# A fused adaLN attention block: engine order from a list scheduler, 4-head sets, exponentials in groups of three and two banks

## The chip, the cores and the metric

One core of a Trainium2 chip. The metric is device time in microseconds (us) of one execution; lower is better. The kernel before has a median of 1135.11 us over three runs (1132.73 to 1136.46). Engines: PE is TensorE (PEld its weight loads), ACT is ScalarE, DVE is VectorE, POOL is GpSimd, SP is SyncE, which here only issues transfers. Some words: PSUM is the memory that TensorE writes to, here in banks of 512 columns; an eviction copies a result out of it; the stationary is the operand that a weight load puts into the array, whose largest form in these profiles has 128 rows and 128 columns (`128*128`); a row or column group is, in these kernels, a strip of 32 of these; the granted clock is the share of full speed that the profile records for TensorE.

## The reference, cut to what matters

```python
# x: 1 x 2048 x 640, 32 heads of 20, gated MLP of 1536, all bfloat16
mod = silu(c) @ w_mod                       # six vectors: sa, ca, ga, sb, cb, gb
h = layernorm(x) * (1 + ca) + sa
q, k, v = split(h @ wqkv)                   # 32 heads x 20
o = softmax(q @ k.T / sqrt(20)) @ v         # 32 x 2048 x 2048 exponentials
x = x + ga * (o @ wo)
h = layernorm(x) * (1 + cb) + sb
x = x + gb * (((h @ w_gate) * (h @ w_up)) @ w_down)
```

The 134 million exponentials go through ScalarE: in the kernel before, one instruction of 128 x 1536 of them lasts 1.45 us alone and follows the last after 1.347 us back to back, and that sets the floor. The heads are small: 20 of the 128 rows of the TensorE array are enough for one head's scores.

## The kernel before

Heads are taken three at a time, in 11 sets. One step is one key tile of 128 for one set and 512 queries: three score matmuls side by side in row groups of the array, one exponential over three PSUM banks, three matmuls with the values (PV) side by side in column groups. The profile has 0.39 us for the three score matmuls together and 0.39 us for the three of PV (at 700.85 and 701.17 us). Each head's 20 rows are padded with zeros to 32, and the score matmul contracts all 32.

```python
SETS = [tuple(range(i, min(i + 3, H))) for i in range(0, H, 3)]
VW = 24                                     # one ones column, 20 values, padding
...
fn = lambda e, ...: e.matmul(
    ps_all[:, bs * 3 + i, :],
    KT_sb[32 * s:32 * s + 32, sg, kt * 128:(kt + 1) * 128],      # 32 rows x 128 columns
    QT_sb[32 * s:32 * s + 32, sg, cq * 512:(cq + 1) * 512],
    tile_position=(32 * s, 0))
...
fn = lambda e, ...: e.activation(Pbuf[:, sl, 0:nh * 512], ps_sflat[bs][:, 0:nh * 512],
                                 ACT.Exp, scale=SCALE)
```

All other matmuls (projections, and for the 512 queries before: out-projection and MLP) are put between the steps. In a step without any, a matmul of no use keeps TensorE occupied:

```python
xs.filler = lambda e: e.matmul(ps_all[:, BXW, :], KT_sb[0:32, 0, 0:128], QT_sb[0:32, 0, 0:512],
                               tile_position=(0, 0))
...
if used == 0:
    if self.filler is not None and step >= self.round_end_step + 2 and self.cur is None:
        self.pe.ins(lambda e, f=self.filler: f(e), waits=...)
```

The softmax here doesn't subtract the row's maximum and nothing guards it: scores larger than these inputs give would overflow.

## Time and profile before

| | us | how to read it |
|---|---|---|
| median of three runs | 1135.11 | |
| span of the profiled run | 1138.6 | first to last instruction |
| until the first exponential | 91.4 | head: load, modulation, layer norm, projections |
| exponentials | 969.5 | stream; 921 at the pace of ScalarE, 48.5 of stalls |
| after the last exponential | 77.7 | tail: the last queries' out-projection and MLP |

The lines that carry this are in the prediction. Two more will matter. The first is from the slices of the page of the kernel before: the TensorE clock that was granted, in tenths, in 40 slices of the span. The second is from its costliest groups: the score matmuls, with busy time, the mean of one in ns, and the idle time before them.

### The profile page before, as it was taken

How to read it: one execution, taken by the hardware profiler on the slowest of the kernel's cores; microseconds unless marked ns; L12 is line 12 of the kernel's file. 1: busy time of each engine (PE TensorE's matmuls, PEld its weight loads, DVE VectorE, ACT ScalarE, POOL GpSimd, SP SyncE). 2: the span in 40 equal slices, each digit the busy share in tenths (PEclk: the TensorE clock that was granted, in tenths of full speed). 3: DMA queues.
4: the chain of work that ended last, by engine and by line, in shares of the span. 5: the costliest groups of instructions: out<-in, count | busy, mean ns of one | idle time of the engine just before them, and what ended most of it. 6: DMA issues, size and time to landing. Idle time of an engine off the chain costs nothing.

```text
span 1138.6 us, 14720 instructions
## 1 busy us (share of the span) xinstructions
PE 952.1 (84%) x6035; PEld 293.7 (26%) x6095; DVE 390.4 (34%) x690; ACT 969.7 (85%) x752; POOL 37.8 (3%) x52
## 2 busy tenths in 40 slices
PE   1677898899998888888997898889987888889778
PEld 0331222222222222222322222223222222223434
DVE  2741322344323333332114333321123333322475
ACT  1559999999999899999999999999987999999200
POOL 7000000000000000000000000000000000000000
PEclk9788999999989889898989779999977899989889
DMA  8100001000022001100230011100400011100422
GB/s 295 57 1 1 1 1 30 1 1 1 1 75 53 1 12 45 37 13 6 68 78 1 1 30 41 35 1 18 133 1 1 12 36 35 24 6 20 126 64 64
DMA packets 80418, 40.59 MB, mean 36 GB/s; under 512 B 64544, under 2 KB 80032, under 8 KB 80352
## 3 DMA queue, kind: packets, MB, share of 16 engines
q1 hardware_dynamic: 77328, 32.29, 11.0%
q10 hardware_dynamic: 2624, 4.92, 1.2%
q0 software_dynamic: 400, 2.46, 0.6%
q8 instruction: 48, 0.79, 0.3%
q14 instruction: 18, 0.15, 0.0%
HBM read 37.03 MB, written 2.62 MB: 35 GB/s over the span
## 4 chain that ended last, share of the span: by engine, by line
PE 39%; ACT 29%; issue 16%; DVE 13%; POOL 2%; another core or an unknown queue 0%; ACTq 0%; POOLq 0%
ACT Pbuf L1146 26%; PE ps_all L1159 9%; PE ps_all L1130 9%; PE ps_all L724 7%; PE ps_all L959 3%; PE ps_all L1036 3%; PE ps_all L1073 3%; PE ps_all L1049 2%; PE ps_all L746 2%; DVE OT L1183 2%; DVE KT_sb L734 1%; DVE QT_sb L734 1%; ACT hT L620 1%; PE ps_all L852 1%; DVE xn L990 1%
## 5 line engine op out<-in xcount | busy, mean ns | idle before, releaser
L1146 ACT ACTIVATE Pbuf<-ps_all 128x1536 bf16<-128x1536 f32 (+1 forms) x704 | 928.9, 1526 | 40.6 <-PE ps_all L1130 39.4
L1130 PE MATMUL ps_all<-QT_sb,KT_sb 32*128 32x512 bf16 x2048 | 296.1, 412 | 73.1 <-ACT Pbuf L1146 49.5
L1159 PE MATMUL ps_all<-Pbuf,V_sb 128*24 128x512 bf16 x2048 | 294.1, 412 | 9.0 <-DVE OT L1183 8.8
L1130 PEld LDWEIGHTS ps_all<-QT_sb,KT_sb 32*128 32x128 bf16 x2048 | 68.9, 92 | 323.7 <-ACT Pbuf L1146 244.2
L1159 PEld LDWEIGHTS ps_all<-Pbuf,V_sb 128*24 128x24 bf16 x2048 | 67.2, 89 | 189.4 <-issue 169.0
L959 PE MATMUL ps_all<-wo_sb,Oc 128*128 128x320 bf16 x352 | 76.7, 344 | 13.9 <-DVE h2T L1005 11.7
L1036 PE MATMUL ps_all<-h2T,wgst 128*128 128x512 bf16 x216 | 71.9, 410 | 9.8 <-DVE hprod L1054 4.4
L1073 PE MATMUL ps_all<-wd_sb,hprod 128*128 128x320 bf16 x384 | 72.5, 313 | 6.2 <-DVE wd_sb L934 5.4
L1049 PE MATMUL ps_all<-h2T,wust 128*128 128x512 bf16 x228 | 71.8, 398 | 4.9 <-DVE gsb L1041 3.4
L1183 DVE STREAM_TRANSPOSE OT<-ps_all 96x512 f32<-96x512 f32 (+1 forms) x44 | 31.3, 711 | 118.3 <-PE ps_all L1159 118.3
L1041 DVE COPY gsb<-ps_all 128x512 f32<-128x512 f32 x48 | 32.9, 685 | 89.8 <-PE ps_all L1036 82.4
L1054 DVE TENSOR_TENSOR hprod<-ps_all,gsb 128x512 bf16<-128x512 f32 x48 | 32.8, 684 | 89.9 <-PE ps_all L1049 78.8
L968 DVE TENSOR_TENSOR xck<-ps_all,xck 128x320 bf16<-128x320 f32 x32 | 15.3, 486 | 121.5 <-PE ps_all L959 121.5
L746 PE MATMUL ps_all<-Wv,hT 128*128 128x384 bf16 x160 | 40.6, 394 | 12.9 <-ACT hT L620 12.9
L1083 DVE TENSOR_TENSOR xck<-ps_all,xck 128x320 bf16<-128x320 f32 x32 | 15.5, 484 | 98.5 <-PE ps_all L1073 98.5
L724 PE MATMUL ps_all<-hT,Wk 128*128 128x512 bf16 x147 | 43.5, 394 | 6.3 <-DVE KT_sb L734 2.9
L724 PE MATMUL ps_all<-hT,Wq 128*128 128x512 bf16 x149 | 42.8, 383 | 5.3 <-issue 1.0
L734 DVE CAST KT_sb<-ps_all 128x512 bf16<-128x512 f32 x32 | 22.1, 691 | 67.1 <-PE ps_all L724 67.1
L959 PEld LDWEIGHTS ps_all<-wo_sb,Oc 128*128 128x128 bf16 x352 | 29.2, 106 | 51.8 <-issue 22.7
L734 DVE CAST QT_sb<-ps_all 128x512 bf16<-128x512 f32 x32 | 22.1, 692 | 56.0 <-PE ps_all L724 53.9
L1073 PEld LDWEIGHTS ps_all<-wd_sb,hprod 128*128 128x128 bf16 x384 | 30.3, 99 | 38.4 <-issue 17.9
L934 DVE TENSOR_TENSOR wd_sb<-wd_sb,mods_b 128x640 bf16<-128x640 bf16 x48 | 39.0, 813 | 0.0
(68 smaller groups left out, 433.5 us busy)
## 6 DMA issues: line engine op xcount, KB each, us to landing
wd_sb<-in_B_w_down_dram SPq DMA_DIRECT2D x4, 1920.0 KB, 9.4
wgst<-in_B_w_gate_dram SPq DMA_DIRECT2D x48, 160.0 KB, 2.7
wust<-in_B_w_up_dram SPq DMA_DIRECT2D x48, 160.0 KB, 2.8
wmod_sb<-in_w_mod_dram ACTq DMA_DIRECT2D x4, 1200.0 KB, 13.9
x<-in_A_x_dram SPq DMA_DIRECT2D x4, 640.0 KB, 7.1
xck<-in_A_x_dram SPq DMA_DIRECT2D x4, 640.0 KB, 4.3
out_dram<-xck SPq DMA_DIRECT2D x16, 160.0 KB, 1.8
wraw<-in_A_wqkv_dram POOLq DMA_DIRECT2D x5, 480.0 KB, 5.9
```

The lines of the kernel that those rows point to most:

```text
L724: fn = lambda e, b, kt=kt: e.matmul(psbank(b), Wx[:, kt, sg, :], hT[:, tc, kt, :], start=(kt == 0), stop=(kt == KT - 1))
L734: eve = dve.ins(lambda e: e.tensor_copy(dst[:, sg, tc * 512:(tc + 1) * 512], psbank(b)), inc=c_ev, waits=w)
L746: fn = lambda e, b, kt=kt: e.matmul(psbank(b)[:, 0:ncol], hT[:, tc, kt, (t % 4) * 128:(t % 4 + 1) * 128], Wv[:, kt, cc * ncol:(cc + 1) * n ...
L934: ev_wdp_l[0] = dve.ins(lambda e: e.tensor_tensor(wd_sb[:, fc, :], wd_sb[:, fc, :], mods_b[:, 2, :], ALU.mult), inc=c_ev, waits=[ev_wdl])
L959: fn = lambda e, b, j=j, tl=tl, nch=nch: e.matmul(ps_all[:, b, 0:320], Ocq[:, j, tl * 128:(tl + 1) * 128], wo_sb[:, j, nch * 320:(nch + 1) ...
L1036: fn = lambda e, b, kt=kt, stg=stg: e.matmul(psbank(b), wgst[:, stg, kt, :], h2T[:, kt, :], start=(kt == 0), stop=(kt == KT - 1))
L1049: fn = lambda e, b, kt=kt, stg=stg: e.matmul(psbank(b), wust[:, stg, kt, :], h2T[:, kt, :], start=(kt == 0), stop=(kt == KT - 1))
L1073: fn = lambda e, b, fc=fc, tl=tl, nch=nch: e.matmul(ps_all[:, b, 0:320], hprod[:, fc, tl * 128:(tl + 1) * 128], wd_sb[:, fc, nch * 320:(nc ...
L1130: fn = lambda e, bs=bs, i=i, sg=sg, s=s, cq=cq, kt=kt: e.matmul(ps_all[:, bs * 3 + i, :], KT_sb[32 * s:32 * s + 32, sg, kt * 128:(kt + 1) ...
L1146: fn = lambda e, sl=sl, nh=nh, bs=bs: e.activation(Pbuf[:, sl, 0:nh * 512], ps_sflat[bs][:, 0:nh * 512], ACT.Exp, scale=SCALE)
L1159: fn = lambda e, i=i, h=h, sl=sl, kt=kt: e.matmul(ps_all[32 * i:32 * i + VW, BO, :], V_sb[:, kt, h * VW:(h + 1) * VW], Pbuf[:, sl, i * 512 ...
L1183: ev_t1 = dve.ins(lambda e, rows=rows: e.transpose(OT[0:rows, :], ps_all[0:rows, BO, :]), inc=c_at, waits=[ev_pv[g], st["onorm"]] + extra)
```

## The change

The intent: fewer and fuller instructions, and an order of every engine that is worked out at build time by a list scheduler which knows the engines' durations. Heads go in eight sets of four; score tiles flow in one queue into groups of three banks (A) and two banks (B) in turn; queries and keys are projected packed (five blocks of 128 rather than eight padded ones) and laid out by small transfers from SBUF to SBUF ("relays"); the out-projection contracts 5 blocks of 128 instead of 11 sets; the modulation is folded into evictions and weights; the head of the program does only what the first scores need. The scores contract 20 rows now, the values' stationary has 21 columns, and there is no filler. The core of the diff (2,680 lines, all else cut):

```diff
-    SETS = [tuple(range(i, min(i + 3, H))) for i in range(0, H, 3)]
-    NSET = len(SETS)
+    NSET = 8
...
-    xs.filler = lambda e: e.matmul(ps_all[:, BXW, :], KT_sb[0:32, 0, 0:128], QT_sb[0:32, 0, 0:512],
-                                   tile_position=(0, 0))
...
-                KT_sb[32 * s:32 * s + 32, sg, kt * 128:(kt + 1) * 128],
+                dstf()[:, i * u.n:(i + 1) * u.n], KT[32 * u.s:32 * u.s + DH, u.j, kt * 128:(kt + 1) * 128],
+                QT[u.ci][32 * u.s:32 * u.s + DH, u.j, :], tile_position=(32 * u.s, 0)))
...
+    GA = [0, 1, 2]
+    GB = [3, 4]
```

## The prediction

> **What bounds the kernel now.** I read the page's busy shares and slices first, then the costliest groups, the chain, the timelines of ScalarE, and last the stretches by window.
>
> ```profile
> PE 952.1 (84%) x6035; PEld 293.7 (26%) x6095; DVE 390.4 (34%) x690; ACT 969.7 (85%) x752; POOL 37.8 (3%) x52
> ...
> ACT  1559999999999899999999999999987999999200
> ...
> PE 39%; ACT 29%; issue 16%; DVE 13%; POOL 2%; another core or an unknown queue 0%; ACTq 0%; POOLq 0%
> ...
> L1146 ACT ACTIVATE Pbuf<-ps_all 128x1536 bf16<-128x1536 f32 (+1 forms) x704 | 928.9, 1526 | 40.6 <-PE ps_all L1130 39.4
> ```
>
> Two engines are near 85%, but the slices tell them apart: ScalarE is at 7 to 9 tenths in 34 slices running and nearly idle at both ends. The run is three stages: a head, a stream of exponentials, a tail. The chain of waits names PE more than ACT only because inside the stream the two hand work to each other every step; the 928.9 us of exponentials are what can't shrink.
>
> ```profile
> 90.12 1.28 ACT L1146 ACT_TABLE_LOAD   x1
> 91.41 4.13 ACT L1146 ACTIVATE Pbuf<-ps_all 128x1536 bf16<-128x1536 f32 x3
> ...
> 428.70 45.90 ACT L1146 ACTIVATE Pbuf<-ps_all 128x1536 bf16<-128x1536 f32 x34
> 475.11 1.45 ACT L1146 ACTIVATE Pbuf<-ps_all 128x1536 bf16<-128x1536 f32 x1 [0.51 <-PE ps_all L1130]
> ...
> 1057.05 3.87 ACT L1146 ACTIVATE Pbuf<-ps_all 128x1024 bf16<-128x1024 f32 x4
> ```
>
> The stream runs from 91.4 to 1060.9 us: head 91.4, stream 969.5, tail 1138.6 - 1060.9 = 77.7. A 1536-wide exponential alone lasts 1.45 us; back to back they come every (45.90 - 1.45)/33 = 1.347 us. For 1024 wide I take 1.347 less 512 x 0.833 ns = 0.92 (three steps of the last row give (3.87 - 1.02)/3 = 0.95). So the stream's floor is 640 x 1.347 + 64 x 0.92 = 921 us, and 48.5 us of it are stalls (40.6 shown as idle).
>
> Where the stalls lie, in the stretches of the exponential line alone (columns: stretch, its length, ACT busy, granted clock, DMA share, GB/s):
>
> ```profile
> 240.00:290.00 50.00, 50.00 (x38) 1.00 0.00 1
> ...
> 340.00:390.00 50.00, 43.98 (x33) 0.84 0.18 42
> ...
> 840.00:890.00 50.00, 41.52 (x31) 0.80 0.00 1
> ```
>
> They gather just after each 512-query chunk, where PE carries the out-projection of the chunk before, and where the granted clock falls to 0.80-0.84.
>
> [...]three score matmuls take 0.39 us together. [...]In the trace scores, PV and full matmuls start 0.32 us after one another (700.84, 701.17, 701.49), against 0.216 us for a full matmul in the tail's unbroken rows (1.08 us for five). [...]The page's issues show 1.8 us for a store and 2.7 us for a gate tile; issuing costs 12.80/32 = 0.4 us each for the 20-row loads of wo.
>
> **The change part by part.**
>
> *Stream, work of ScalarE.* 2048 score tiles of 512 in groups of 3 and 2 alternately: 410 exponentials of 1536 and 409 of 1024. Floor: 410 x 1.347 + 409 x 0.92 = 929 us, 8 us worse than before; 115 more instructions pay the fixed part.
>
> *Stream, stalls.* The five banks instead of six free two for the other matmuls (before: one). PE gets lighter: K/Q packed, 42 rounds of five against 64 (22 x 1.08 = 24 us less); out-projection contracts 5 blocks of 128 rather than 11 sets (352 to 160 matmuls of 320 columns, at 3.15/22 = 0.143 us from the tail's rows, 27 us less); 83 filler matmuls go (18 us); PV comes in batches of 7 to 8 on four column groups, about 256 batches rather than 704 sets of three[...]. Against it: the three-bank group must be refilled within one 0.92 us exponential. The release needs 0.05 us and scores to exponential 0.47 us (scores at 202.79, exponential at 203.26), and the exponential may be late by the ~0.1 us the pipeline overlaps; that leaves 0.3-0.4 us of slack in which PE may be in something else. The listing of the new PE order shows full matmuls and PV batches put mostly into the longer window, but it is fixed at build time and the clock isn't: at 0.80, blocks stretch by a quarter. I take 3% of the stream: 28 us, against 48.5.
>
> *Head.* Removed: large memsets, 60 mod matmuls before layer norm with broadcast copies, the clearing of Oc on ScalarE (11 us, 79-90), the sqrt table, and waiting for all four x chunks. New order by DVE and PE rows: x and the first mod slices land at ~10 us (x landed at 11.2 behind larger loads), the second mod slice ~13.5 (at the 400 GB/s of the first loads). Stats 8 x 0.4, aggregate 0.4, pow on POOL ~1, four xn 1.5: xn at ~18. Transposes and five evacuations to ~20.5. Then six projection rounds precede the first scores; two at the cold clock (2.1 us), four at 1.08, plus an evacuation of 0.69: first exponential at ~30. Six exponentials (7 us of work) use the first 512 keys. The keys of the second chunk come only after DVE has done, in its order, 14 statistics (5.6), four V evacuations (2.0), five hT evacuations (2.1), eight xn (3.0), aggregates and pow waits (3) on top of the chunk's own statistics (6): ~21 us, then 2-3 us by DMA. So the second batch starts at ~54.5. After that DVE needs ~5 us for each chunk of keys and ScalarE 7.3, and the relay's 7-8 issues of 0.4 us (3 us a block) just keep up. Effective start of the stream: 54.5 - 7.5 = 47 us, against 91.4.
>
> *Tail.* Last PV 0.7; transpose, reciprocal, multiply, transpose 2.4; relay of O by DMA 5 x 0.4 + 2 = 4. Out-projection is then bound by DVE: for each tile two adds and two statistics at 0.4-0.49, aggregate 0.2, xn 0.45 (the two 0.82 us modulation passes are folded into the evacuation): 4 x 2.5 = 10, plus 1 for the last pow and 0.7 for the first round; transposes 3; gate/up 24 x 1.08 = 26; down 13.2 as now; add and store 2.5. Sum 63.5, against 77.7.
>
> *Sum.* 47 + 929 + 28 + 63.5 = 1067.5 as a span; the timed runs before lie 3.5 us under their profile (1135.1 to 1138.6), so 1064. The stalls are the softest term, and my head estimate counts every DVE row in series, so I shade to 1060.
>
> **Rivals.** *The tight refill wins:* each three-bank refill comes 0.2 us late; 410 x 0.2 = 82 us of stalls eat all that the stream could gain, and the time is ~1115. For it: PE already made ScalarE wait in 66 places with 1.34 us windows. Against: most of those have three full matmuls after PV or a low clock, and PE's load falls by about 80 us. *The relay starves the first items:* some 150 small K/Q DMAs wait in one queue in program order[...]; if a block takes 5 us rather than 3, items 1 to 3 wait and the head's gain is halved: ~1085. For it: 0.4 us an issue leaves no margin early on. Against: four staging slots, and later blocks have 29 us per item. *Everything hides:* stalls of 8 us and a head of 42: ~1035. *ScalarE's extra instructions only:* the smaller groups alone would cost 8 us, never a loss beside the head and tail, so a slower result needs stalls over 140 us.
>
> **Range and chances.** Head 42-58, stalls 8-50, tail 59-68 about a floor that is nearly sure; taken as partly independent they give 1037 to 1085 around 1060 us. Faster by over 2% means under 1112: 0.96. Within 2%: 0.03. Slower: 0.01.
>
> **What would show it.** Right: exponentials of 1536 and 1024 still at 1.45 and 1.02 us alone and 1.347 and 0.92 apart; their busy time about 935 us; a first exponential near 30 us, a gap of ~15 us after the sixth, the stream ending near 1004; a tail of 63 with gate/up back to back. Wrong: idle before the three-bank group of 0.2 us at every turn (first rival); PE scores waiting for DMA of KT past 60 us (second); a first exponential after 40 us, or an exponential row clearly slower than 1.347.

What the traces show of the rates that it uses: in the kernel before, a lone exponential lasts 1.451 us for 1536 columns and 1.024 us for 1024, which makes 0.83 ns a column ((1451 - 1024) / 512) and a fixed part of 0.17 us (3 x 1.024 - 2 x 1.451); back to back, the median end of a 1024-wide one is 0.916 us after the end of the one before it, so the 0.92 holds. Five full matmuls of 512 columns take 1.08 us at full clock; at half clock they start 0.40 to 0.43 us apart in the changed kernel, so five take 2.0 to 2.1 us. The first loads of the kernel before moved 395 GB/s from 10 to 15 us. Its transfers of 160 KB landed 1.8 us (store), 2.7 us (gate) and 2.8 us (up) after their issue; the profile has no landing times for the small relays. The relay of O in the tail of the changed kernel took 4.3 us from its first issue (1131.50 us) to the matmul that waited for it (1135.76 us), where the prediction has 4.

## More of the kernel before

```profile
PEclk9788999999989889898989779999977899989889
...
L1130 PE MATMUL ps_all<-QT_sb,KT_sb 32*128 32x512 bf16 x2048 | 296.1, 412 | 73.1 <-ACT Pbuf L1146 49.5
```

The clock is a little under full in many slices, 7 in the lowest; its mean over the run is 0.913. (The time before the first record of the clock, here 28.6 us, counts as full in all these rows and means, though it wasn't: a matmul of 320 columns took 474 ns at 25 us and 299 ns at 30 us.) The form `32*128` says that 32 rows and 128 columns of the array are in use.

## The result, and the profile after

| | before | after |
|---|---|---|
| median, us | 1135.11 | 1206.59 |
| range, us | 1132.73 to 1136.46 | 1199.04 to 1220.20 |
| mean granted TensorE clock, profiled run | 0.913 | 0.689 |

Ratios in this document are the mean time of one kernel's fast runs over that of the kernel before's fast runs of the same rounds, so they are not quite the ratio of the medians. Here the ratio is 1.0615, with a 95% interval of 1.0555 to 1.0675: **slower by 6%**, where 6.6% faster was predicted. One of the four runs (1220.20) counts as slow and is left out of it.

The page of the changed kernel: busy shares, slices, the chain of waits by engine, and the costliest groups of the stream (busy time, mean ns; idle time before, and its releaser).

```profile
PE 1018.2 (85%) x5709; PEld 258.6 (22%) x5770; DVE 276.2 (23%) x529; ACT 963.3 (80%) x837; POOL 45.9 (4%) x67
...
ACT  1278988878989898889979999986999998779611
...
PEclk9598965556555575579755688765657687559679
...
PE 54%; ACT 29%; issue 10%; DVE 4%; DMA 1%; POOL 1%; SPq 1%; POOLq 0%; ACTq 0%; DVEq 0%
...
L942 ACT ACTIVATE PA<-ps_all 128x1536 bf16<-128x1536 f32 x410 | 608.1, 1483 | 142.4 <-PE ps_all L917 140.9
L917 PE MATMUL ps_all<-QT,KT 20*128 20x512 bf16 x2048 | 415.2, 513 | 125.8 <-ACT PA L942 86.5
L942 ACT ACTIVATE PB<-ps_all 128x1024 bf16<-128x1024 f32 x409 | 433.0, 1059 | 12.5 <-PE ps_all L917 10.3
```

Two things stand out. TensorE is busy for *longer* than before, 1018 us instead of 952, with some 325 fewer matmuls: a score matmul takes 513 ns on average, not 412. And the clock row, 7 to 9 before, is full of fives. The chain of waits names PE for 54% of the span, 39% before, and the slices of ScalarE hold eights and sevens where the kernel before has nines. The exponential of three banks waits 142 us for its scores, that of two banks 12. That is just the pattern that the first rival of the prediction foretold (the tight refill), so the lines alone don't tell whether the grouping or the clock is at fault.

The trace by stretches says more. Columns: stretch, its length, busy time (and instructions) of PE, PEld, DVE, ACT and POOL, granted clock, DMA share, GB/s.

```profile
100.00:150.00 50.00, 47.09 (x346) 16.10 (x349) 17.46 (x31) 48.36 (x44) 7.26 (x5) 0.98 0.09 23
300.00:350.00 50.00, 41.77 (x210) 7.71 (x209) 9.38 (x17) 44.22 (x39) 17.52 (x14) 0.50 0.28 75
343.00:393.00 50.00, 45.93 (x243) 9.21 (x235) 12.45 (x28) 45.77 (x39) 3.19 (x8) 0.50 0.01 2
800.00:850.00 50.00, 49.17 (x242) 12.87 (x241) 5.82 (x11) 37.13 (x31) 0.00 (x0) 0.57 0.04 14
1000.00:1050.00 50.00, 45.61 (x208) 8.26 (x205) 7.90 (x12) 40.51 (x35) 0.00 (x0) 0.53 0.13 30
```

At a clock of 0.98 the stream makes 44 exponentials in 50 us, 2.27 us for a pair: exactly the predicted floor, 1.347 + 0.92, with every wait of the new order in it. At 0.50 to 0.57 it makes 39, 39, 31 and 35. TensorE is busy for 42 to 49 of the 50 us there, yet the clock stays at half or near it; the longest spell, 123 us on end from 293 us, covers the second and third of these stretches. The matmuls' own records agree with the clock: a score matmul lasts 0.39 us at full clock and 0.60 us at half. In this trace the clock has two values, 1.0 and 0.5, and changes at steps of 3.41 us (the 123 us are 36 of them). In those 123 us TensorE never sits idle for more than 2.0 us and is busy for 41 to 46 of every 50 us, and the clock stays at half. In the stretches above it is busy for 47 of 50 us at a clock of 0.98 and for 49 at 0.57, so its busy time alone doesn't explain the clock.

The head, from the timeline of ScalarE of the changed kernel (start, length, what, and in brackets the idle time before it):

```profile
29.93 1.45 ACT L942 ACTIVATE PA<-ps_all 128x1536 bf16<-128x1536 f32 x1 [8.96 <-PE ps_all L917]
...
36.33 1.02 ACT L942 ACTIVATE PB<-ps_all 128x1024 bf16<-128x1024 f32 x1 [0.43 <-PE ps_all L917]
68.61 1.45 ACT L942 ACTIVATE PA<-ps_all 128x1536 bf16<-128x1536 f32 x1 [31.26 <-PE ps_all L917]
```

The first exponential is at 29.9 us (predicted: about 30), and six run; the second batch starts at 68.6 instead of 54.5. Put into the prediction's own terms (effective start = second batch less 7.5 us; floor 929; the rest of the stream is stalls):

| term, us | predicted | after | difference |
|---|---|---|---|
| effective start of the stream | 47 | 61.1 | +14 |
| floor | 929 | 929 | 0 |
| stalls | 28 | 138.2 | +110 |
| tail | 63.5 | 69.0 | +5 |
| span | 1067.5 | 1197.2 | +130 |

### The profile page after: what moved, and what is told of

The parts are those of the page before. It is cut to its first block, busy times and chain, and to the rows that moved or that the text cites. A ratio compares the mean times of both kernels' runs of the same rounds, so it can differ in the third digit from the quotient of the medians.

```text
span 1197.2 us, 14624 instructions
## 1 busy us (share of the span) xinstructions
PE 1018.2 (85%) x5709; PEld 258.6 (22%) x5770; DVE 276.2 (23%) x529; ACT 963.3 (80%) x837; POOL 45.9 (4%) x67
## 4 chain that ended last, share of the span: by engine, by line
PE 54%; ACT 29%; issue 10%; DVE 4%; DMA 1%; POOL 1%; SPq 1%; POOLq 0%; ACTq 0%; DVEq 0%
PE ps_all L917 18%; ACT PA L942 17%; PE ps_all L1298 12%; ACT PB L942 12%; PE ps_all L1186 9%; PE ps_all L688 5%; PE ps_all L1216 4%; PE ps_all L1114 3%; PE ps_all L770 2%; DMA x<-in_A_x_dram 1%; DVE st L627 1%; PE ps_all L1146 1%; SPq L1065 1%; DVE st L1129 0%; DMA Ocp<-OcT 0%
## 5 line engine op out<-in xcount | busy, mean ns | idle before, releaser
L942 ACT ACTIVATE PA<-ps_all 128x1536 bf16<-128x1536 f32 x410 | 608.1, 1483 | 142.4 <-PE ps_all L917 140.9
L917 PE MATMUL ps_all<-QT,KT 20*128 20x512 bf16 x2048 | 415.2, 513 | 125.8 <-ACT PA L942 86.5
L942 ACT ACTIVATE PB<-ps_all 128x1024 bf16<-128x1024 f32 x409 | 433.0, 1059 | 12.5 <-PE ps_all L917 10.3
L1298 PE MATMUL ps_all<-PA,V 128*21 128x512 bf16 x1230 | 237.7, 523 | 0.3 <-ACT PA L942 0.3
L1298 PE MATMUL ps_all<-PB,V 128*21 128x512 bf16 x818 | 234.9, 526 | 0.6 <-DVE V L776 0.6
L917 PEld LDWEIGHTS ps_all<-QT,KT 20*128 20x128 bf16 x2048 | 79.5, 96 | 494.7 <-ACT PA L942 228.1
L1186 PE MATMUL ps_all<-h2T,stg 128*128 128x512 bf16 x353 | 142.0, 504 | 2.2 <-issue 2.1
L1216 PE MATMUL ps_all<-wd,hprod 128*128 128x320 bf16 x384 | 81.8, 345 | 0.8 <-DVE hprod L1201 0.8
L688 PE MATMUL ps_all<-hT,wraw 128*128 128x512 bf16 x178 | 72.7, 515 | 3.4 <-DVE st L627 1.0
L1114 PE MATMUL ps_all<-wo,Ocp 128*128 128x320 bf16 x160 | 43.1, 408 | 12.3 <-DMA Ocp<-OcT 11.9
```

The costliest lines, as they stand in the source:

```text
L688: f = lambda e, b, k=k: e.matmul(bank(b), wraw[:, k, base + b5 * 128: base + b5 * 128 + 128], hT[:, k, tc * 512:(tc + 1) * 512], start=(k ...
L917: ems.append(lambda e, i=i, kt=kt: e.matmul(dstf()[:, i * u.n:(i + 1) * u.n], KT[32 * u.s:32 * u.s + DH, u.j, kt * 128:(kt + 1) * 128], QT ...
L942: return e.activation(pbuf[:, cellp["p"], 0:nu * 512], ps[:, b0:b0 + nu, :].rearrange("p b c -> p (b c)"), AFT.Exp, scale=ESCALE)
L1114: f = lambda e, b, k=k, tl=tl, hf=hf: e.matmul(ps[:, b, 0:320], Ocp[:, slot, k, tl * 128:(tl + 1) * 128], wo_sb[:, k, 320 * hf:320 * hf + ...
L1186: f = lambda e, b, k=k, cell=wbuf[w_]: e.matmul(ps[:, b, 0:n], cell["t"][:, k, :], h2T[:, k, 0:n], start=(k == 0), stop=(k == KD - 1))
L1216: f = lambda e, b, fc=fc, tl=tl, hf=hf: e.matmul(ps[:, b, 0:320], hprod[:, fc, tl * 128:(tl + 1) * 128], wd_sb[:, fc, 320 * hf:320 * hf + ...
```

## The experiments

Fifteen kernels ran; all gave the right result. Those of one group ran on the same chip beside the kernel before. A run counts as slow when it is over 1.5% above the fastest of the same kernel. Medians and ranges (in brackets) are of all runs.

### Is it the clock, and what does the clock follow?

The theory at first (H1): the change took so much work off the array that its activity fell under what keeps the clock at full, activity being the area in use, rows times columns times time. Rivals: plain busy time of TensorE decides (H2); the tight refill stalls by itself (H3); the 83 fillers alone kept the kernel before warm (H5).

**fill_full.** Matmuls of no use in the idle time of TensorE, chosen by the scheduler so that no score group is due:

```diff
-        return False
+        return filler(t)
+    def filler(t):                                   # at most two per score group
+        ...
+        e.matmul(ps[0:128, cell["b"], 0:512], ident[0:128, 0:128], fz[0:128, 0:512], start=True, stop=True)
```

> The changed kernel with 540 filler matmuls (full 128x128 stationary, 512 columns, about 0.22 us each at full clock) put into idle TensorE time of the exponential stream, at most two per exponential; nothing else differs and their results are never read. Theory H1 (the loss is the TensorE clock, and the clock follows the array area that is streamed, rows times columns times time): the area per 3.41-us window rises from a lowest 0.15 to a lowest 0.33 of the array, above which the changed kernel's trace hardly ever fell to half clock; so mean clock 0.93 or more and 1075 to 1100 us (a stream near its 929-us floor plus some 30 us, the head's late second batch and the 69-us tail kept). Rival H2 (plain busy time of TensorE decides): about the same, it differs in the next run. Rival H3 (the tight 0.92-us refill of the three-bank group stalls by itself): clock may rise but the time stays at 1180 or more, since the fillers take TensorE time from the refill.

**fill_rows20.** The same at the same places, with 20 rows (in these two cuts the numbers stand for the program's constants):

```diff
+        e.matmul(ps[0:128, cell["b"], 0:512], ident[0:20, 0:128], fz[0:20, 0:512], start=True, stop=True)
```

> The same fillers at the same places, as long, but with a stationary of 20 rows instead of 128: they add TensorE busy time and almost no array area (0.034 us of full array each instead of 0.216). H1 (area decides): the lowest windows stay at about 0.2 of the array, the clock stays at 0.75 or less and the time at 1190 us or more, likely above the changed kernel's 1206 since the fillers cost 0.43 us each at half clock. H2 (plain busy time decides): same as the full fillers, clock 0.93 or more and 1075 to 1100 us.

**before_rows20.** The kernel before, with the zero padding left out of the contraction:

```diff
-                KT_sb[32 * s:32 * s + 32, sg, kt * 128:(kt + 1) * 128],
-                QT_sb[32 * s:32 * s + 32, sg, cq * 512:(cq + 1) * 512],
+                KT_sb[32 * s:32 * s + 20, sg, kt * 128:(kt + 1) * 128],
+                QT_sb[32 * s:32 * s + 20, sg, cq * 512:(cq + 1) * 512],
```

> The kernel before with its score matmuls contracting 20 rows instead of 32 (the 12 rows left out are zero padding, the result is the same): the same number of instructions of the same length, 3/8 less array area in the scores. H1: the stretches without projection work go from 0.21 of the array to about 0.16, as in the changed kernel; clock down from 0.91 to 0.75 to 0.85 and time up to 1150 to 1190 us. H2 and H3: no change, 1135 us within 0.5%, clock 0.91.

**before_nofill.** The kernel before without its fillers:

```diff
-            if self.filler is not None and step >= self.round_end_step + 2 and self.cur is None:
+            if False and self.filler is not None and step >= self.round_end_step + 2 and self.cur is None:
```

> The kernel before without its 83 filler matmuls (32 rows, 512 columns, issued only in steps without other extra work). Theory H5 (these fillers alone keep the kernel before warm and their removal is the loss): clock down to 0.8 or less and time up 3% or more. H1: 83 fillers of a quarter of the array are some 4.5 us of array in 1000 us, so little changes: clock 0.88 to 0.91, time 1135 to 1148 us.

| run | median, us | clock, profiled run | ratio to before (95%) |
|---|---|---|---|
| fill_full | 1116.22 (1102.88 to 1120.75) | 0.924 | 0.978 (0.971 to 0.985) |
| fill_rows20 | 1305.66 (1293.06 to 1313.37) | 0.632 | none given |
| before_rows20 | 1229.97 (1215.54 to 1237.01) | 0.777 (fast runs 0.786 to 0.803) | 1.078 (1.071 to 1.085) |
| before_nofill | 1136.36 (1135.50 to 1139.61) | 0.896 | 1.000 (0.997 to 1.003) |

H2 falls at once: the same fillers at the same places give 1116 us with 128 rows and 1306 with 20. The page of fill_rows20, busy share of TensorE and the clock by slices:

```profile
PE 1208.7 (93%) x6249; PEld 296.0 (23%) x6310; DVE 275.6 (21%) x529; ACT 979.8 (76%) x837; POOL 45.9 (4%) x68
...
PEclk9589955555555555558765555657857577556779
```

TensorE is busy for 93% of the span and cold for most of it. The mirror image is before_rows20, from its page the clock and the score matmuls:

```profile
PEclk9789979999956568959755565999666565989889
...
L1130 PE MATMUL ps_all<-QT_sb,KT_sb 20*128 20x512 bf16 x2048 | 343.5, 470 | 43.5 <-ACT Pbuf L1146 24.1
```

Nothing but twelve rows of zeros was taken out of each score matmul of the kernel before, and it became 8% slower (I had expected at most 5%, and its profiled run is slow). So a loss of this size needs neither the scheduler nor the grouping nor the relays. H5 falls too: without its fillers the kernel before is as fast as with them.

fill_full came in 16 us over the expected range. From its page the clock, and the stretch that explains it (columns as above):

```profile
PEclk9697999999999999999855569999999999999889
```

```profile
550.00:600.00 50.00, 48.53 (x216) 10.67 (x212) 10.14 (x22) 36.79 (x31) 2.38 (x6) 0.50 0.01 2
```

After 103 us the stream has one cold spell, from 540 to 653 us (the expectation of fill_pad below has 551 to 651), with some 50 of the fillers inside it, about as many as in the 113 us before: once cold, it stayed cold for 113 us. In this trace returning took more activity than staying.

**pad_only.** No filler; the scores contract 32 rows and the values' stationary has 32 columns (of the next head, outputs never read):

```diff
+    pvw = VW if (4 * u.j + s) % 16 == 15 else 32
-                KT[32 * u.s:32 * u.s + DH, u.j, ...], QT[u.ci][32 * u.s:32 * u.s + DH, u.j, :]
+                KT[32 * u.s:32 * u.s + 32, u.j, ...], QT[u.ci][32 * u.s:32 * u.s + 32, u.j, :]
-                ps[32 * s:32 * s + VW, BPV, 0:u.n], V[:, kt, (4 * u.j + s) * VW:(4 * u.j + s + 1) * VW]
+                ps[32 * s:32 * s + pvw, BPV, 0:u.n], V[:, kt, (4 * u.j + s) * VW:(4 * u.j + s) * VW + pvw]
```

The padding rows of keys and queries are zeroed once, on GpSimd.

> The changed kernel with no filler at all, but with the contraction of the scores padded from 20 to 32 rows (the 12 rows are zeroed once) and the values' stationary widened from 21 to 32 columns (the 11 extra output rows are never read): the same TensorE instructions at the same length, only more rows and columns of the array in each. The area in the stretches without projection work goes from 0.15 to about 0.24 of the array, what the kernel before has there with its fillers. H1 (area decides): clock 0.85 to 0.93 and 1090 to 1140 us, from 1206. H2 (busy time decides) and H3 (the refill of the three-bank group stalls by itself): no change, 1195 to 1215 us at a clock of 0.69.

**fill_cols20.** The fillers with 128 rows and 20 columns:

```diff
+        e.matmul(ps[0:20, cell["b"], 0:512], ident[0:128, 0:20], fz[0:128, 0:512], start=True, stop=True)
```

> The 540 fillers with 128 rows but only 20 columns: same length, same row count as the full ones, a small area. If the clock followed the rows alone, the result would be that of the full fillers (1103 to 1121 us at 0.91 to 0.92); if area (H1), that of the 20-row fillers (1293 to 1313 us at 0.63). I expect the second.

**fill_pad.** Full fillers and both paddings.

> Full fillers and padding together. The lowest windows of the stream then have 0.40 of the array and more, and even at half clock the pace of the stream would give about 0.6, above the 0.55 from which the traces show a return to full clock, so that the one cold spell of 100 us that the fillers alone had (551 to 651 us, some 32 us lost) should be gone or short. H1: clock 0.95 or more, 1065 to 1085 us, the runs closer together than those of the fillers alone.

| run | median, us | clock, profiled run | ratio to before (95%) |
|---|---|---|---|
| pad_only | 1135.53 (1130.90 to 1140.12) | 0.796 | 0.998 (0.992 to 1.003) |
| fill_cols20 | 1114.57 (1086.45 to 1143.67) | 0.932 | 0.979 (0.974 to 0.984), two fast runs of six |
| fill_pad | 1076.15 (1070.68 to 1077.30) | 0.976 | 0.944 (0.940 to 0.949) |

pad_only takes 71 us off the changed kernel without one TensorE instruction more; its time is in the expected range, its clock of 0.796 under the expected 0.85 to 0.93. But fill_cols20 is a miss that mattered: I expected the 20-column fillers to do no more than the 20-row ones (about 1300 us), and they do as much as the full ones: its fast runs, 1086.45 and 1098.43, are at or under the full fillers' 1102.88 to 1116.96. (Four of its six runs are slow, at clocks of 0.865 to 0.897 against 0.918 and 0.932; nothing is built on those. The medians of all runs, 1114.57 and 1116.22 us, agree too.) Area is wrong: in the fillers the columns don't count, the rows do.

So the theory became H1r: **what counts is the share of the array's 128 rows that is being fed, over time**. To see whether that holds window by window I took, in every 3.41-us window of 17 traces, each matmul's streaming time (the traces have about 0.22 us for 512 columns at full clock and 0.43 at half), and from it three measures: the share of time with any matmul (busy), rows times columns (area), and rows alone, where matmuls that feed different rows side by side add up and those that feed the same rows at the same time count once (fed rows). Then I asked which one tells best whether the next window has another clock, with the threshold at which the two shares of error together are smallest:

| at full clock (3642 windows that stay, 296 that drop) | best threshold | stay, though below it | drop, though above it |
|---|---|---|---|
| busy | 0.52 | 7.9% | 5.7% |
| area | 0.37 | 8.0% | 3.4% |
| fed rows | 0.41 | 3.9% | 0.7% |

| at half clock (1157 that stay, 303 that return) | best threshold | stay, though above it | return, though below it |
|---|---|---|---|
| busy | 0.765 | 56% | 6% |
| area | 0.585 | 29% | 5% |
| fed rows | 0.69 | 19% | 7% |

Fed rows is the best of the three in both directions. It is a fit, not a specification: the ends of matmuls are modelled in the trace, and other weightings were not tried to the end. A recount with another program, from the same traces past 50 us, gave 0.39 and 0.71 for fed rows, with errors of 2.5% and 0.3% at full clock and of 8% and 8% at half. It also tried one more rival, the data streamed in, where each matmul counts though others feed the same rows beside it: errors of 11% and 5% at full clock, and 81% and 2% at half, so it is no better than busy. By the fit, about 0.41 is enough to stay warm and about 0.69 is needed to become warm, which would explain the stubborn cold spells. No run was made to test these two thresholds.

**pad_rows** and **pad_cols** test the other half of the theory, that rows count and columns don't: the two halves of pad_only, one at a time.

> After the 20-column fillers worked as well as the full ones, the theory is amended to H1r: what counts is the share of the array's 128 rows that are fed at a time, summed over time, whatever the number of columns; matmuls that feed the same rows at the same time count once. Here only the scores' contraction is padded to 32 rows, the values' stationary keeps its 21 columns. H1r: all of the gain of the two paddings together, 1130 to 1142 us and a clock near 0.80. Area (H1): between the changed kernel and both paddings, 1150 to 1185 us.

> Only the values' stationary is widened from 21 to 32 columns, the scores keep 20 rows. H1r: nothing, 1199 to 1220 us and a clock of 0.66 to 0.70. Area (H1): 1150 to 1185 us.

| run | median, us | clock, profiled run | ratio to before (95%) |
|---|---|---|---|
| pad_rows | 1134.47 (1124.42 to 1138.13) | 0.801 | 0.996 (0.991 to 1.001) |
| pad_cols | 1213.17 (1203.15 to 1224.21) | 0.682 | 1.063 (1.058 to 1.069) |

The rows carry all of the gain and the columns none. The clock by slices, first pad_rows, then pad_cols:

```profile
PEclk9788987667756589699866596899757699999589
```

```profile
PEclk9597965566555578569755688659556665568679
```

**H3, the tight refill**, is settled by fill_pad. From its page:

```profile
PEclk9778999999999999999999999999999999999889
```

```profile
L962 ACT ACTIVATE PA<-ps_all 128x1536 bf16<-128x1536 f32 x410 | 696.3, 1698 | 46.0 <-PE ps_all L937 45.8
L962 ACT ACTIVATE PB<-ps_all 128x1024 bf16<-128x1024 f32 x409 | 520.8, 1273 | 1.0 <-PE ps_all L937 1.0
```

Of the 46.0 us of idle time before the three-bank group, 41.2 are the two waits of the head (9.7 before the first exponential and 31.6 before the seventh); 5 us are left for the other 400. In the changed kernel it is 142.4 less 9.0 and 31.3, so 102. (The means of the exponentials are higher because their records overlap when they follow back to back: the two sums, 696.3 and 520.8 us, make 1217 us, and ScalarE was busy for 938.1 us in all.) In the prediction's terms the stalls are 1000.9 - 67.3 - 929 = 4.6 us, although TensorE has more to do than in the changed kernel. At full clock the refill is in time, but for these few us in the whole run.

### What is the change worth with the clock taken out?

**before_warm** gives the kernel before two fillers of 128 rows in each of its idle steps (240 instead of 83); **before_warm2** three at each of the original 83 places.

```diff
-            if self.filler is not None and step >= self.round_end_step + 2 and self.cur is None:
-                self.pe.ins(...)
+            if self.filler is not None and step > self.round_end_step and self.cur is None:   # before_warm2: >= ... + 2
+                for _ in range(2):                                                            # before_warm2: range(3)
+                    self.pe.ins(...)
-    xs.filler = lambda e: e.matmul(ps_all[:, BXW, :], KT_sb[0:32, 0, 0:128], QT_sb[0:32, 0, 0:512],
-                                   tile_position=(0, 0))
+    xs.filler = lambda e: e.matmul(ps_all[:, BXW, :], KT_sb[0:128, 0, 0:128], QT_sb[0:128, 0, 0:512])
```

> The kernel before with its own fillers changed to 128 rows and issued twice in every step that has no other extra work (240 instead of 83): what the kernel before takes at a warm clock, so that the change can be judged with the clock taken out. Its 0.91 leaves a few short cold spells, each of which costs some us: H1r expects a clock of 0.95 or more and 1100 to 1130 us, so that the changed kernel, warm, is still faster by 3 to 5%. If it lands at 1075 us or below, the change is worth nothing in itself.

> The kernel before with three fillers of 128 rows at each of the 83 places of its own fillers, where no wait on an eviction is in the way (the first control put fillers where the only spare bank was still being read, and TensorE waited 41 us for it). With a clock of 0.94 or more: 1110 to 1135 us, so the warm changed kernel at 1071 to 1077 us is 4 to 5% faster at like clock. If this control reaches 1090 us or less, most of the gain of the warm changed kernel is the clock and little the change.

Both are misses: 1174.39 us (1170.94 to 1178.52), ratio 1.033 (1.029 to 1.037), and 1158.65 us (1153.13 to 1161.55), ratio 1.020 (1.015 to 1.024). The clock rises to 0.936 and 0.939, but the kernel before has one spare bank and a fixed order of steps, and the fillers come where scores are due. In before_warm they also wait for the bank to be read, from the groups of its page:

```profile
L852 PE MATMUL ps_all<-QT_sb,KT_sb 128*128 128x512 bf16 x240 | 77.5, 407 | 41.4 <-DVE hprod L1053 16.2
```

So there is no measured warm time of the kernel before. An estimate can be had from its own profile: if all its 48.5 us of stalls went, it would have a span of 91.4 + 921 + 77.7 = 1090 us, and fill_pad is at 1069. This is no bound, for its head and tail ran partly at half clock too (mean 0.80 from 28.6 to 91.4 us, 0.89 in the tail). What the change is worth at equal clock stays open.

### The head and the tail

The second batch of scores needs the keys of the second 512 tokens. **head1** moves the value rounds behind the next key round, issues every second relay of the first key block on ScalarE's queue and puts fillers in the head; **head2** has one queue again and holds the other key and query blocks of the first chunk back behind the sixth exponential, for their staging slots, and two weight loads; **head3** gives the staging eight slots instead of four, holds only what isn't needed early, and moves the padding's zero fills; **head3t** has fillers in the tail too. All have fillers and padding.

```diff
-            v_round(t, 0, 14 + 20 * tc)
+            v_round(t, 0, 35 + 20 * tc if tc < 3 else 74)                  # head1, head2, head3, head3t
-    load_wm(2, wm_b[0], "sp", 8, x0_done)
+    load_wm(2, wm_b[0], "sp", 8, x0_done, gate=60)                         # head2: 30
-    NKS = 4
+    NKS = 8                                                                # head3, head3t
-        lim = FCAP
+        lim = 60 if g <= 12 else 80 if g >= NG else FCAP                   # the 80: head3t, until the gate rounds
```

> As the run before, and the head reworked: the value rounds of a sequence chunk are issued after the next chunk's key round, the first key block's relays are issued on two queues, and fillers keep the clock up from the start to the second batch of scores. In the changed kernel the second batch's first exponential starts at 68.6 us; if its lateness comes from the cold clock (46 to 70 us at half clock), the value rounds ahead and the relays' issue one after another, it moves to 56 to 62 us and the time to 1055 to 1077 us, 6 to 12 below the run before. If it hangs on the landing of data alone, it stays at 66 us or later and the time is that of the run before.

> Fillers and padding, and the head reworked again after the first try moved the second batch only from 74.8 to 70.7 us: in that trace the first relayed key block had its matmuls done at 51 us but its eviction waited on VectorE until 57.2 us, behind the statistics of two more chunks, because its four staging slots were taken by blocks that nothing needed yet; and two 800-KB weight loads of the modulation ran beside its relays from 58 to 64 us. Here those other blocks come after the sixth exponential and the two loads after the thirtieth; relays stay on one queue. If that is what the gap in the head is, the second batch starts at 56 to 62 us and the time is 1058 to 1068 us; if the relay itself is (issue and landing), it stays near 70 us and the time near 1073 us.

> The head for the third time, with fillers and padding. The traces of the first two showed: the zero fills of the padding on GpSimd stretched four VectorE normalisations from 1.52 to 7.34 us and moved the first exponential from 30 to 36 us; and when blocks were held back, the relays stood in one queue at 0.94 us each, so that the second item's query block landed at 97 us, with 12.5 us of ScalarE idle before it. Here the zero fills lie before the normalisations (GpSimd) and on idle ScalarE, there are eight staging slots instead of four, so early relays leave early and no eviction waits for a slot, the third key block and two modulation loads come after the sixth and the sixtieth exponential. Expected: first exponential at 30 to 31 us, second batch at 54 to 60 us, the 40th exponential before 102 us (116 in the run with fillers and padding alone), 1050 to 1062 us. If the relays' issue rate bounds the head whatever the order, the 40th exponential stays at 110 us or later and the time at 1065 us or more.

> The same with fillers also between the last score group and the first gate round of the tail, where the run with fillers and padding still fell to half clock twice (10 and 7 us). If the tail's excess over the predicted 63.5 us is the cold clock, 3 to 6 us less than head3; if it is the relay and the chain of normalisation, the same as head3 within 1 us.

| run | median, us | first / seventh / 40th exponential | end of stream | tail | ratio to before (95%) |
|---|---|---|---|---|---|
| changed kernel | 1206.59 | 29.9 / 68.6 / 110.0 | 1128.3 | 69.0 | 1.062 (1.056 to 1.068) |
| fill_pad | 1076.15 | 36.4 / 74.8 / 115.5 | 1000.9 | 68.0 | 0.944 (0.940 to 0.949) |
| head1 | 1072.73 | 36.0 / 70.7 / 111.6 | 1001.5 | 68.8 | 0.943 (0.939 to 0.946) |
| head2 | 1075.62 | 35.7 / 60.6 / 115.3 | 1003.3 | 67.9 | 0.945 (0.943 to 0.948) |
| head3 | 1067.73 | 31.2 / 60.3 / 103.1 | 998.3 | 68.5 | 0.940 (0.937 to 0.943) |
| head3t | 1063.49 | 30.5 / 59.6 / 98.9 | 998.3 | 64.0 | 0.935 (0.931 to 0.939) |

head1 is a miss for the second batch (70.7, not 56 to 62), with a time in its wide range, but 3.4 us below fill_pad and not 6 to 12. It showed two causes. The eviction of the first relayed key block, done by TensorE at 51 us, ran at 57.2: it stood in VectorE's order behind the statistics of two more chunks. And the padding had made the head later by 6 us. The normalisations of the first chunk on VectorE, first in fill_full, then in fill_pad, where a zero fill runs on GpSimd from 15.1 us on:

```profile
15.17 1.52 DVE L648 TENSOR_SCALAR xn<-x,mv,rs 128x640 bf16<-128x640 bf16 x4 [1.49 <-POOL rs L640]
```

```profile
15.12 7.34 DVE L653 TENSOR_SCALAR xn<-x,mv,rs 128x640 bf16<-128x640 bf16 x4 [1.49 <-POOL rs L644]
```

The same four instructions take 7.34 us instead of 1.52 while the zero fills run (fill_pad has them on GpSimd from 15.14 to 25.52 us, fill_full has nothing there). Not all of VectorE's work was held up: two evictions at 23.17 and 24.42 us, beside the last fills, took 0.54 and 0.55 us, as in fill_full. What in the fills stretched the normalisations was not shown; with the fills out of the way (head3) the first exponential is back at 31.2 us, from 36.4.

head2 moved the seventh exponential to 60.6, as expected, and gained nothing, as I had not expected: the held-back blocks then stood in one long queue. Its transfer queue (start, length, transfers), and ScalarE where it waited for them:

```profile
48.64 46.03 SPq L733 DMA_DIRECT2D KT<-Kst  x49
94.77 5.11 SPq L733 DMA_DIRECT2D QT<-Kst  x7
```

```profile
98.17 1.02 ACT L963 ACTIVATE PB<-ps_all 128x1024 bf16<-128x1024 f32 x1 [12.53 <-PE ps_all L938]
```

A relay takes 0.94 us of the queue here (46.03 / 49), and the next item's queries come after 49 of them. This is the second rival of the prediction, the relay that starves the first items; whether the issuing or the transfers behind it set that pace was not separated. head3 relieves it in part (40th exponential at 103.1, just over the expected 102; its time 1067.73 us above the expected 1050 to 1062), and the rest of the head's loss stays open: up to the 40th exponential the queue issues relays without a break.

head3t against head3 is the tail: 64.0 us instead of 68.5, as expected, with 4.2 us less in the median. From the page of head3t, the clock:

```profile
PEclk9999989999989999999999999999999999999999
```

**head3t is faster than both kernels**: 1063.49 us (1058.39 to 1064.44) against 1134.10 us of the kernel before in the same rounds.

## Why the prediction was wrong

**What held.** The division into head, stream and tail; the floor of 929 us (2.27 us for a pair wherever the clock is full); the first exponential at 30 us; six exponentials before the gap; the refill of the three-bank group, whose slack of 0.3 to 0.4 us is enough. The tail of 63.5 us is 64.0 once it is warm.

**The step that failed: "I take 3% of the stream: 28 us."** The stalls were 138 us. The prediction had seen the clock (0.80 to 0.84 in two stretches of the kernel before), but took it as a given with which the work is to be multiplied, "at 0.80, blocks stretch by a quarter", and counted all lightening of TensorE as gain: 24 us of projection, 27 of out-projection, 18 of fillers. It doesn't mention the one that weighs most, the contraction of the scores over 20 rows instead of 32: put back alone, in pad_rows, it takes the changed kernel from 1207 to 1134 us, the time of the kernel before. In these runs the clock was an outcome of that very work: its mean was 0.689 in the changed kernel and 0.801 in pad_rows. A count from the traces suggests by how much (estimates, from the 0.216 us that the traces have for a full matmul of 512 columns in an unbroken row). Between rounds of other work, a step of the kernel before feeds 96 of 128 rows for 0.216 us with three score tiles, and all rows for 0.216 us with PV: 0.378 us in 1.347, so 0.28. A pair of groups after feeds 60 and 40 of 128 rows for 0.216 us each, and PV has five tiles, of which 7 to 8 share two turns of 0.216 us: 0.169 + 0.288 = 0.457 us in 2.27, so 0.20. Both are under the 0.41 of the fit and by it need other rounds beside them to stay warm. The change has over a quarter less of it in itself, and fewer other rounds to add. Once cold, at the 3.23 us for a pair that 31 exponentials in 50 us make, the same work, twice as long at half clock, makes 0.28; by the fit the return takes 0.69, so it would need a long row of full matmuls. The cold spells of the kernel before last 3 to 14 us, those of the changed one up to 123 us. (That these estimates explain each spell is argued from the fit; what the runs show is that rows alone move the clock and the time.) Nothing on the page before warns of this except the clock row itself; the warning sign would have been that a kernel with TensorE busy for 84% of the span isn't at full clock.

**The rival that looked right and wasn't.** "The tight refill wins: each three-bank refill comes 0.2 us late; ~1115." The lines show the idle time where it was foretold, 102 us over 410 groups. fill_pad, with the same grouping and more work on TensorE, has 5. The refill was late because its matmuls ran at half clock.

**The head: second batch at 54.5.** It came at 68.6. Three sizes were off. All but two projection rounds were taken at full clock; from 33.4 to 60.7 us it was half (the expectation of head1 has 46 to 70), and five 320-column matmuls took 1.51 us (0.85 in the warm traces). The eviction of the key block came at 54.7 in VectorE's order. And a relay, whose issue was taken from the weight loads as 0.4 us, holds the changed kernel's transfer queue for 0.74:

```profile
55.85 5.21 SPq L726 DMA_DIRECT2D KT<-Kst  x7
```

The rival "the relay starves the first items" was right in kind: it named 5 us for a block, and the line has 5.2. It was given too little weight. But the three together made the second batch 14 us late, far less than the 110 us of stalls.

**The tail: 63.5.** 69.0, of which head3t takes back 4.5 with a warm clock.

**Two sums of the prediction.** "The timed runs before lie 3.5 us under their profile" compares a median with one execution: in every run the time is about 2 us above the span of the same execution (1199.04 and 1197.2 us in the changed kernel's profiled run), so 1067.5 us of span would be some 1069.5 of time. And "a slower result needs stalls over 140 us" doesn't follow from its terms: 47 + 929 + 63.5 leave 99 us of stalls up to the span of 1138.6 before, and some 122 up to 2% more. 138 were enough for 6%, with the head and tail later too.

**The whole.** With the clock kept up and the head mended in part, the change gives 1063 us where 1060 was predicted. The agreement is partly luck (the stalls are then 17 us and the start at 52), but the terms are the right ones; what the prediction left out is that the change itself removes the condition under which they hold. The chance of 0.01 for slower was far too small for a change that takes, by its own count, some 70 us of work off an engine whose clock, in these runs, depended on its work.

## What to carry to other kernels

When a change takes work off TensorE, estimate the rows of the array that stay fed per window, not only the time saved: by the fit to these traces, which no run tested, the clock halves below some 0.41 and coming back takes about 0.69. This change was to save 6.6% and cost 6%. Zero padding of the contraction and fillers of 128 rows, put where no score group is due, are worth 11% in the changed kernel (1207 to 1076 us), though the padding's zero fills cost 6 us of its head; fillers at fixed places cost the kernel before 2 to 3%. Dropping twelve rows of zeros from the contraction was no free saving here: it made the kernel before 8% slower (1136 to 1230 us). And idle time of one engine before another's work shows who is late, not why: look at the clock of the stretch before blaming the order.
